# One list orders every engine: the same 2710 steps in a new order

## The chip, the cores and the metric

The kernel runs on one core of a Trainium2 chip. The metric is the device time of one execution in microseconds; lower is better. A core has a matrix engine (TensorE, PE in the profile, with PEld for its weight loads), VectorE (DVE), ScalarE (ACT), GpSimd (POOL), and SyncE (SP), which here only issues DMAs. Each engine works through its own queue in the order in which the program names its instructions, and waits at the first one whose inputs or buffers are not ready.

## The reference

Two parts run one after the other. The first is a gated recurrence (an mLSTM) over 768 positions for 4 batches and 8 heads of width 40. Per step it computes

```python
m_new  = np.maximum(f_gate[:, :, t] + m, i_gate[:, :, t])
f_stab = np.exp(f_gate[:, :, t] + m - m_new)
i_stab = np.exp(i_gate[:, :, t] - m_new)
C = f_stab * C + i_stab * outer(v_t, k_t)
n = f_stab * n + i_stab * k_t
y[:, :, t] = sigmoid(o_gate_t) * (C @ q_t) / np.maximum(np.abs(n . q_t), 1.0)
```

The second is a gated feed-forward layer (FFN) on the 3072 tokens of width 320: `(sigmoid(x @ w_gate) * (x @ w_val)) @ w_out`, with 1536 hidden units. The weights arrive as 64-bit floats, the rest as 32-bit floats.

## The kernel before

**Tiles and stages.** The recurrence is computed in 6 chunks of 128 positions. A chunk of one batch is a *unit*; units 0 to 23 are numbered chunk by chunk, four batches each (`unit`, L507). A unit loads q, k, v and the output gate (`lq`, `lk`, `lv`, `lo`) and, from unit 2 on, a decay table (`ld`); turns q and k with PE (`tr`); forms the scores of its heads (`s`, in three groups); multiplies them with the decay table on DVE (`t`); multiplies with V (`av`); adds the contribution of the earlier chunks (`in`, `ti`, `ad`); normalizes (`nd`, `ns`, `ro`, `xd`); turns the result (`xt`) and splits it into a high and a low part (`xh` on ACT, `xl` on DVE) for the FFN. All but the last chunk also update the state (`kw`, `cs`, `cm`, `cd`, `ca`).

How scores get their operands depends on the chunk. In chunks 0 and 1, ACT or DVE copies the turned q and k (`cp`), and q is multiplied with a mask into a block form (`qb`). From chunk 2 on (units 8 to 23) both are split (`kh` on ACT, `kl` on DVE), written to DRAM by six DMAs (`sw`) and read back in another arrangement by four (`sr`), and only then can `s` begin.

**The weights** come as 64-bit words and are unpacked: a load (`wd`), one ACT step (`wa`), three DVE steps (`wb`, `wc`, `wo`), then the high part on ACT (`wh`) and the low part on POOL (`wl`). The letter behind says which weight: `g` gate, `v` value, `r` the rest rows of both, `o` output.

**The FFN** (`ffn`, L852) has 103 pieces. Each has six matmuls for the gate and six for the value (`u0`, `u1`, L863), two more for each (`r0`, `r1`, L867 and L868), tanh on ACT (`th`), the product on DVE (`gx`), the split (`gh` on ACT, `gl` on DVE), and three down-projection matmuls per token tile (`dn`, L897 to L899). The last piece of a chunk is followed by the output copy and store (`ob`). Gate and value have one accumulation bank each, so the next piece's `u0` waits for `th` and its `u1` for `gx`. Pieces 0 to 15 belong to chunk 0, 16 to 39 to chunk 1, and so on; the last chunk's 24 pieces begin with 79.

**What sets the order.** Every step is a small function under a name such as `u1.14` or `sw9.02`. `ORDER` (L36) is one long list of these names, written out in the program; `emit` calls them in turn, and the engines' queues follow that order (no scheduler reorders them). Some buffers rotate, three each for q, k, v, the output gate and the decay table: which load gets which buffer follows the list as well.

**The start.** Gate values are loaded (`lf` on SP, `li` on ACT's queue), scanned (`ga`, `gb`, `gc`, `gm`) and turned (`tap`, `tac`). `i0` to `i6` make masks on POOL. `wm` is 16 warm-up matmuls on zeros. `lq0` is the one q load that ACT's queue issues; all other loads are SP's. Units 0 and 1 get their decay table from PE (`sp`), ACT (`ee`) and POOL (`em`).

Of the kernel before, what the change touches and what calls it, by code (L numbers as in the profile page):

```python
# [13 lines left out]
ALU = mybir.AluOpType  # L14
# [27 lines left out]
    tr2.1 wbo0 xd0 cp2.1 wbo1 wco1 qb2.1 whg0 nd1 wdv1 ns1 wco0 cm0.1 xt0 xh0 ro1 ld3 qb2.0 woo0 xd1 lq3 woo1 ee2.0
    xt1 xl0 wdg1 lo2 lo3 who0 wlg0 xh1 xl1 u0.0 gm4 gm5 r0.0 who1 ee3.1 wlo1 u1.0 th0 wdo2 kw1 r1.0 cs1 wlo0 wag1
    wbg1 og3 tr2.2 gs1 wao2 wdr1 lq5 lv2 wav1 l12 gx0 gh0 cm1.0 cm1.1 wcg1 zs1 gl0 wbv1 wog1 wbo2 gd whg1 em2 wco2
    lk3 ld4 dl2 kw2 u0.1 u1.1 tr3.0 wdg2 cp2.2 tr3.2 lv5 qb2.2 cp3.0 tr3.1 cp3.2 og2 cp3.1 qb3.0 wlg1 s2.1 s2.0 woo2
    who2 tab t2.1 r0.1 wlo2 war1 wag2 l13 zs0 t2.0 tbp tbc lk4 r1.1 dn0.1 qb3.1 wcv1 wbr1 zs2 th1 s2.2 t2.2 cs2
    cm2.1 cm2.0 av2 dn0.0 gx1 gh1 wov1 whv1 wlv1 qb3.2 lo6 wcr1 wbg2 tdp wor1 tdc wdo3 u0.2 ld5 wdv2 nd2 wao3 ns2
    tep gl1 dn1.1 s3.1 dn1.0 ro2 xd2 ee3.0 em3 wbo3 u1.2 wco3 whr1 dl3 wlr1 wdr2 woo3 who3 wlo3 tec t3.1 ee4.1 s3.2
    lq4 ee4.0 s3.0 war2 t3.2 wcg2 r0.2 t3.0 wog2 th2 r1.2 xt2 xh2 xl2 av3 whg2 wbr2 kw3 wlg2 gx2 ns3 gh2 tr4.0 wav2
    u0.3 nd3 ro3 u1.3 r1.3 xd3 gl2 cp4.0 r0.3 wdv3 th3 wbv2 qb4.0 gx3 wdo4 xt3 cs3 xh3 gh3 dn2.0 xl3 cm3.0 cm3.1  # L50
    u0.4 u1.4 wao4 r0.4 r1.4 wcv2 gl3 wov2 dn2.1 whv2 dn3.0 th4 dn3.1 u0.5 wcr2 wor2 lo4 og4 wlv2 gx4 tr4.2 gh4
    ee5.0 gl4 tr4.1 wdg3 lk5 wbo4 whr2 r0.5 u1.5 wco4 r1.5 wdo5 th5 cp4.1 dn4.2 em4 dl4 wlr2 gx5 woo4 gh5 lq6 lv6
    gl5 u0.6 dn4.3 wao5 wbo5 wco5 r0.6 cp4.2 wdr3 th6 who4 wlo4 u1.6 r1.6 qb4.2 dn5.2 wav3 woo5 dn5.3 s4.0 lv4 l14
    kw4 gx6 who5 gh6 wlo5 wbv3 u1.7 u0.7 r0.7 r1.7 wag3 l15 gl6 th7 wcv3 cs4 gx7 wdg4 wov3 dn6.2 war3 dn6.3 wbg3
    whv3 wbr3 t4.0 wlv3 cm4.1 cm4.0 u0.8 u1.8 ld6 s4.2 r0.8 gh7 ee6.1 gl7 ee6.0 wcg3 qb4.1 wdg5 th8 s4.1 t4.2 in4
    wog3 wdo7 r1.8 wcr3 wao7 whg3 ti4 wlg3 ee5.1 gx8 gh8 t4.1 u0.9 dn7.3 tr5.0 lk6 wdv4 wav4 cp5.0 u1.9 tr5.1 wbo7
    wco7 woo7 lk7 who7 tr5.2 wor3 wdo6 gl8 dn7.2 cp5.1 dn8.1 whr3 r0.9 av4 wlo7 r1.9 wbv4 cd4.1 th9 gx9 u0.10 cd4.0
    em5 ad4 ns4 gh9 qb5.1 lq8 dn8.0 nd4 dn8.3 cp5.2 wlr3 wao6 r0.10 wag4 u1.10 wdo8 qb5.0 gl9 dn9.0 dn9.1 dn9.3
    r1.10 ca4.0 wcv4 gs3 wbo6 wco6 qb5.2 ro4 xd4 dn8.2 dn9.2 gs4 wov4 woo6 th10 wbg4 u0.11 gs2 r0.11 whv4 gs5 wlv4
    gx10 gh10 ca4.1 xt4 gl10 dl5 xh4 who6 wlo6 wdr4 u1.11 r1.11 wcg4 th11 wog4 whg4 s5.1 war4 dn10.0 xl4 s5.2 gx11  # L60
    t5.1 wao8 wlg4 wbo8 dn10.3 wbr4 u0.12 wcr4 s5.0 wor4 wco8 woo8 whr4 wag5 gh11 dn10.2 who8 wlr4 u1.12 wbg5 r0.12
    kw5 r1.12 gl11 lq7 dn10.1 t5.2 in5 wlo8 wcg5 th12 wog5 wdr5 wdo9 gx12 u0.13 em6 dl6 wao9 dn11.1 ti5 u1.13 lo5
    og5 r0.13 wdv5 og6 war5 dn11.2 gh12 whg5 wbr5 r1.13 wlg5 ld7 gl12 ee7.0 t5.0 th13 dn12.2 wcr5 tr6.0 wor5 av5
    wav5 wbo9 wco9 woo9 whr5 dn12.1 cp6.0 cd5.1 qb6.0 wlr5 tr6.1 wbv5 wcv5 wov5 l16 ad5 dn11.0 who9 u0.14 dn12.0
    cp6.1 nd5 wdo11 qb6.1 whv5 ns5 cs5 cm5.1 gx13 wlv5 r0.14 cm5.0 dn11.3 gh13 wlo9 s6.1 dn12.3 gl13 wao11 tr6.2
    t6.1 wdo10 lv7 wao10 th14 wbo10 wbo11 cd5.0 cp6.2 ro5 xd5 u1.14 r1.14 gx14 wco10 woo10 u0.15 gh14 wco11 dn13.0
# [10 lines left out]
    t8.2 t8.0 lo9 r0.22 s8.1 t8.1 th22 dn21.0 r1.22 cd7.1 ca7.1 gx22 xt7 lq10 ob0.3 dl9 xh7 xl7 tr9.2 u0.23 lk10 vb8
    kh9.2 sw9.12 kl9.2 r0.23 gh22 u1.23 r1.23 gl22 in8 dn22.0 th23 gx23 sw9.01 qk9.2 ti8 u0.24 sw9.10 av8.0 da8 db8
    sw9.11 av8.1 av8.2 ad8 cs8 cm8.1 sw9.00 sr9.10 sr9.01 sr9.11 sr9.00 cm8.0 r0.24 ld11 nd8 u1.24 ns8 lk11 dn21.1
    dn22.1 tr10.0 gh23 tr10.1 r1.24 gl23 dn23.0 th24 gx24 dn23.1 kh10.0 kl10.0 kh10.1 sw10.02 ob0.2 kl10.1 u0.25  # L80
    r0.25 u1.25 r1.25 gh24 ea10 qk10.0 kw9 gl24 th25 tr10.2 l19 dn24.1 qk10.1 gx25 u0.26 u1.26 i4 kh10.2 qk10.2
# [869 lines left out]
```

## Time and profile before

| what | value |
|---|---|
| median of 3 runs | 557.59 us (554.11 to 567.98) |
| the profiled execution, whole | 555.66 us |
| its span, first to last instruction | 553.7 us |
| PE busy | 530.0 us, 96% of the span |
| PE weight loads busy | 485.6 us, 88% |
| DVE, ACT, POOL busy | 328.0, 230.1, 246.8 us |
| granted PE clock, mean | 0.99 |
| DMA moved | 72.34 MB, mean 131 GB/s |

The page is one profiled execution. Its second part cuts the span in 40 slices of 13.84 us; a digit is the busy share of a slice in tenths. A line of the chain of waits is a start, a duration and what ran; a line of the waits is who waited for whom, the sum in us, how many times, and the longest one. Matmuls overlap in the array, so busy time of PE counts a matmul's whole passage, not its pace.

### The profile page before, as it was taken

Reading aid. Unit: us, or ns where it says so; the run is one execution under the profiler, and the core shown is the slowest. Engines: PE = TensorE matmul, PEld = TensorE weight load, DVE = VectorE, ACT = ScalarE, POOL = GpSimd, SP = SyncE. Lnnn points to the kernel's source line nnn. Section 1 sums busy time; section 2 is a strip of 40 time slices with the busy share of each in tenths; the row PEclk is TensorE's granted clock in tenths of the full one; section 3 lists DMA queues with packets and bytes.
Section 4 is the critical chain, followed back from the end, with each engine's and each line's share of the span. In section 5 each row is a group of like instructions: output and inputs, shape, how many; then the busy total and the mean of one; then the engine's idle time right before and its main releaser. Section 6 shows DMA issues by size and latency. Waiting matters only on the chain.

```text
span 553.7 us, 10954 instructions
## 1 busy us (share of the span) xinstructions
PE 530.0 (96%) x4101; PEld 485.6 (88%) x4101; DVE 328.0 (59%) x734; ACT 230.1 (42%) x580; POOL 246.8 (45%) x293
## 2 busy tenths in 40 slices
PE   7678999999989999999999999999999999999997
...
DVE  5988877865655564764564654667543554543332
...
PEclk9879999999999999999999999999999999999999
DMA  9897573430787446277786537667047674010000
GB/s 205 228 234 211 135 225 73 134 106 22 179 194 184 125 113 126 58 178 203 171 200 120 114 118 161 177 168 181 25 133 154 147 183 115 27 26 25 25 1 24
DMA packets 131644, 72.34 MB, mean 131 GB/s; under 512 B 103112, under 2 KB 120776, under 8 KB 131592
## 3 DMA queue, kind: packets, MB, share of 16 engines
...
q10 hardware_dynamic: 1088, 0.26, 0.3%
...
## 4 chain that ended last, share of the span: by engine, by line
PE 73%; DMA 9%; DVE 7%; ACT 4%; SPq 2%; issue 2%; POOL 1%; ACTq 0%; DVEq 0%; POOLq 0%
PE pg L863 28%; PE po L897 7%; PE po L899 6%; PE po L898 6%; PE pg L867 5%; PE pg L868 5%; PE av L753 4%; DMA qs<-scr 2%; PE s L664 2%; PE in L736 2%; PE pt L638 2%; PE cs L816 2%; DVE gl L887 1%; PE av L760 1%; PE xt L795 1%
## 5 line engine op out<-in xcount | busy, mean ns | idle before, releaser
L863 PE MATMUL pg<-xh,wh 128*128 128x256 f32 (+1 forms) x412 | 106.3, 340 | 2.0 <-ACT sg L873 1.4
L877 DVE SCALAR_TENSOR_TENSOR sg<-sg,pg 128x256 f32<-128x256 f32 (+1 forms) x103 | 54.1, 525 | 89.0 <-PE pg L868 72.9
L863 PE MATMUL pg<-xl,wh 128*128 128x256 f32 (+1 forms) x412 | 101.6, 328 | 0.0
L863 PE MATMUL pg<-xh,wl 128*128 128x256 f32 (+1 forms) x412 | 101.5, 328 | 0.0
L882 ACT ACTIVATE gh<-sg 128x256 fp32r<-128x256 f32 (+1 forms) x103 | 51.8, 502 | 107.2 <-DVE sg L877 80.8
L897 PE MATMUL po<-oh,gh 128*128 128x320 f32 x288 | 95.8, 332 | 0.0
L899 PE MATMUL po<-oh,gl 128*128 128x320 f32 x288 | 89.7, 311 | 1.0 <-DVE gl L887 1.0
L873 ACT ACTIVATE sg<-pg 128x256 f32<-128x256 f32 (+1 forms) x103 | 48.1, 467 | 101.1 <-PE pg L868 61.1
L898 PE MATMUL po<-ol,gh 128*128 128x320 f32 x288 | 89.2, 310 | 0.0
L887 DVE TENSOR_TENSOR gl<-sg,gh 128x256 fp32r<-128x256 f32 (+1 forms) x103 | 67.2, 652 | 36.5 <-ACT gh L882 36.1
L863 PEld LDWEIGHTS pg<-xl,wh 128*128 128x128 f32 x412 | 69.7, 191 | 7.2
L863 PEld LDWEIGHTS pg<-xh,wl 128*128 128x128 f32 x412 | 69.6, 190 | 7.2
L863 PEld LDWEIGHTS pg<-xh,wh 128*128 128x128 f32 x412 | 67.2, 191 | 5.3 <-ACT sg L873 2.3
L867 PE MATMUL pg<-xh,w 128*128 128x256 f32 (+1 forms) x206 | 70.4, 343 | 0.1
L868 PE MATMUL pg<-xl,w 128*128 128x256 f32 (+1 forms) x206 | 67.3, 328 | 0.0
L709 POOL TENSOR_TENSOR dr<-d 128x1024 f32<-128x1024 f32 x16 | 31.7, 1979 | 61.6 <-DVE d L693 61.4
L897 PEld LDWEIGHTS po<-oh,gh 128*128 128x128 f32 x288 | 54.5, 189 | 2.9
L898 PEld LDWEIGHTS po<-ol,gh 128*128 128x128 f32 x288 | 54.4, 189 | 2.9
L899 PEld LDWEIGHTS po<-oh,gl 128*128 128x128 f32 x288 | 54.2, 188 | 1.7 <-DVE gl L887 1.7
L693 DVE TENSOR_TENSOR d<-s,d 128x384 f32<-128x384 f32 (+1 forms) x72 | 35.5, 508 | 28.1 <-PE s L664 22.2
L593 POOL TENSOR_SCALAR_AFFINE_SELECT d<-d 128x1024 f32<-128x1024 f32 x22 | 25.8, 1175 | 45.7 <-ACT d L589 44.9
L585 POOL TENSOR_TENSOR d<-at,d 128x1024 f32<-128x1024 f32 x16 | 31.8, 1995 | 26.7 <-DMA d<-mscr 19.1
...
## 6 DMA issues: line engine op xcount, KB each, us to landing
d<-mscr SPq DMA_DIRECT2D x22, 512.0 KB
...
k<-in_k_dram SPq DMA_DIRECT2D x24, 160.0 KB
o<-in_o_gate_dram SPq DMA_DIRECT2D x24, 160.0 KB
v<-in_v_dram SPq DMA_DIRECT2D x24, 160.0 KB
su_o<-in_moe_w_out_dram SPq DMA_DIRECT2D x12, 320.0 KB
out_dram<-ob SPq DMA_DIRECT2D x24, 160.0 KB
```

Of the source, the lines that this page charges most:

```text
L585: E("ea", n).tensor_tensor(dm[n], a, dm[n], ALU.subtract)
L693: nc.vector.tensor_tensor(y, ps_[n, g][:, :nh, :], y, ALU.mult)
L863: nc.tensor.matmul(p, w[y][:, a, fs], x[c][:, a, n0:n1], start=(i + a == 0), stop=False)
L867: nc.tensor.matmul(pg[n, y], w2[y][:, fs], xh[c][:, 2, n0:n1], start=False, stop=False)
L868: nc.tensor.matmul(pg[n, y], w2[y][:, fs], xl[c][:, 2, n0:n1], start=False, stop=True)
L873: nc.scalar.activation(s, pg[n, 0], AF.Tanh, scale=0.5)
L877: nc.vector.scalar_tensor_tensor(sgs[n], sgs[n], 1.0, pg[n, 1], ALU.add, ALU.mult)
L882: nc.scalar.activation(ghs[n][:, :nt], sgs[n], AF.Copy)
L887: E("gl", n).tensor_tensor(gls[n][:, :nt], sgs[n], ghs[n][:, :nt].bitcast(F32), ALU.subtract)
L897: nc.tensor.matmul(p, ghs[n][:, ts], oh[:, j, :], start=(j == 0), stop=False)
L898: nc.tensor.matmul(p, ghs[n][:, ts], ol[:, j, :], start=False, stop=False)
L899: nc.tensor.matmul(p, gls[n][:, ts], oh[:, j, :], start=False, stop=(j == NF - 1))
```

## The change

The list is replaced by another one. It holds the same names, each once; what differs is where they stand. The first lines of the old and the new list, and later stretches:

```diff
-    i3 lf li wz lk0 i1 wm lq0 wdv0 i2 ga tap tr0.2 tr0.0 lo1 i0 lq1 gm0 sp1.0 cp0.0 cp0.2 sp0.0 i6 gb tac ee1.0
-    tr0.1 sp0.1 i5 gc qb0.0 em1.0 gm1 gm2 gm3 cp0.1 ee0.0 em0.0 ee0.1 em0.1 lk1 tr1.1 tr1.0 wdr0 lk2 gs0 cp1.0 wav0
-    war0 wdg0 cp1.1 sp1.1 qb0.2 s0.2 tr1.2 qb1.1 ee1.1 lv0 l10 qb1.0 dl0 t0.2 kw0 cp1.2 lq2 s0.0 qb0.1 wag0 s1.0
...
-    xh6 xl6 gl18 r1.19 ee9 tr9.1 dn18.0 sr8.10 sr8.11 th19 u0.20 gx19 r0.20 u1.20 r1.20 kh9.0 kl9.0 sr8.01 kh9.1
...
-    qk11.1 gx32 cm9.1 lk12 da10 u0.33 lv11 lv10 r0.33 u1.33 r1.33 lv12 in10 gh32 gl32 ro9 th33 tr11.2 xd9 gx33
...
-    s23.2 ns22 dn77.3 xt21 xh21 r1.78 dn77.0 t23.2 xl21 dn76.2 da23 th78 u0.79 dn77.1 gx78 r0.79 in23 gh78 nd22 ro22
...
-    dn101.3 dn101.2 gh102 gl102 dn102.3 dn102.2 ob5.3 ob5.2
+    i6 wz li lf i0 wdo0 wao0 wdr0 i3 i2 lq0 lk1 ga gm0 wbo0 wco0 woo0 lq1 wdv0 tap tac sp0.0 war0 i1 gb sp1.1 tr1.1
+    who0 ee0.0 wav0 em0.0 wbr0 gc tr1.0 gm1 wcr0 lk0 cp1.0 cp1.1 qb1.1 lo0 wdo2 tr1.2 zs2 wbv0 cp1.2 gm2 wlo0 wao2
+    lv0 l10 lv1 sp1.0 zs1 gs0 zs0 wor0 ee1.0 em1.0 ee1.1 em1.1 tr0.1 tr0.0 cp0.0 cp0.1 og0 lq3 qb1.0 lk2 sp0.1 tr0.2
+    cp0.2 ee0.1 wcv0 wdg0 em0.1 s1.1 wm ld2 lo2 gm3 gm4 qb0.1 lq2 qb0.0 s0.0 s0.1 qb0.2 s1.0 wbo2 whr0 qb1.2 s0.2
...
+    gl17 cs7 th18 gx18 xh6 xl6 sw8.02 lk10 lv10 gh18 u0.19 r0.19 cm7.0 cd7.0 tr9.0 u1.19 gl18 th19 ea9 r1.19 dn17.0
...
+    gl21 dn21.1 em8 dl8 kw8 u1.22 r1.22 th22 s8.2 t8.2 in8 ti8 cd8.0 dn21.0 s8.1 gx22 gh22 gl22 u0.23 r0.23 em9
...
+    sw23.10 gh77 gl77 u1.78 sw23.00 s22.0 t22.0 u0.78 lo21 og21 av21.0 av21.1 av21.2 ad21 da22 xt20 ns21 dn77.1 lo23
+    nd21 r1.78 xh20 dn77.2 r0.78 th78 ro21 xl20 xd21 dn77.3 sw23.01 xt21 gx78 xh21 xl21 gh78 in22 ti22 dn77.0 vb22
...
+    dn98.2 gh99 gl99 th100 gx100 gh100 dn99.3 gl100 u0.101 r0.101 th101 u1.101 r1.101 dn99.2 gx101 u0.102 gh101
+    r0.102 u1.102 r1.102 dn100.2 dn100.3 gl101 dn101.3 dn101.2 th102 gx102 gh102 gl102 dn102.3 ob5.3 dn102.2 ob5.2
```

Beside the list, the diff adds two parameters and code for another way to move q, k and the FFN's input through DRAM. Its branches are entered for chunks from the parameter on, and both parameters equal the number of chunks:

```diff
+    'QT': 6,
+    'XT': 6,
...
+        bounced = c >= PARAM["QT"]
+        xbounced = c >= PARAM["XT"]
...
-    if PARAM["V32"] < NCH - 1:
+    if PARAM["V32"] + 1 < PARAM["QT"]:
...
+    scq = [dram.tile([2 * DM + 2, L], F32, name=f"scq{n}", tag=f"scq{n}") for n in range(2)]
+    scx = [dram.tile([DM, L], F32, name=f"scx{n}", tag=f"scx{n}") for n in range(2)]
+    rsign = const.tile([P, 6], F32, name="rsign")
...
+        if bounced:
...
-        if not stacked:
+        elif not stacked:
```

More of the change, by code (lines that the diff above doesn't have):

```diff
@@ L42 @@
[L42 to L66, printed above, removed]
@@ L77 @@
[L77 to L81, printed above, removed]
@@ new lines @@
+    r1.1 gl0 th1 dn0.0 t2.2 wdg2 t2.0 gx1 s2.1 ld3 gh1 tr3.2 cp3.2 u0.2 t2.1 war1 wbr1 tbp tbc wag2 wbg2 ee3.1 wcr1
+    gl1 av2 ee3.0 lv4 lo3 cs2 qb3.0 wcg2 wog2 wdo3 wao3 dn0.1 ns2 nd2 em3 dn1.1 ld4 cm2.0 wbo3 wco3 wor1 og3 cm2.1
+    tdp lk4 tdc l13 dn1.0 gs2 dl3 tep ee4.1 ro2 wdv2 xd2 whr1 s3.0 qb3.2 tec wlr1 t3.0 whg2 woo3 wlg2 u1.2 s3.2 s3.1
+    r0.2 th2 t3.2 xt2 xh2 t3.1 xl2 kw3 r1.2 gx2 av3 who3 wlo3 wdr2 war2 wbr2 tr4.0 ns3 u1.3 ee4.0 r1.3 wdv3 nd3 ro3
+    xd3 gh2 gl2 u0.3 r0.3 wav2 th3 xt3 dn2.0 cp4.0 qb4.0 dn2.1 wbv2 xh3 wcv2 cs3 wcr2 gx3 xl3 u1.4 wdo4 wao4 wor2
@@ new lines @@
+    qk17.2 gx58 dn57.1 kl17.2 ca15.0 s16.0 u1.59 r1.59 kl17.1 sw17.12 sw17.11 sw17.10 s16.2 gh58 gl58 dn58.1 dl16
+    t16.2 t16.0 l116 dn57.0 va17 lo16 r0.59 in16 ea17 ee17 ti16 cd16.0 dn57.2 dn58.2 kw16 lo17 dn57.3 s16.1 t16.1
+    da16 th59 gx59 gh59 db16 gl59 cs16 cm16.0 u0.60 r0.60 u1.60 tr18.0 th60 cm16.1 dn58.3 r1.60 og16 u0.61 ca16.0
+    dn59.2 tr18.1 dn59.1 va16 lo18 kh18.0 sr17.10 kl18.0 kh18.1 kl18.1 em17 qk18.0 dl17 sr17.01 qk18.1 gx60 sr17.00
+    dn59.3 dn58.0 dn59.0 gh60 cd16.1 gl60 tr18.2 vb16 av16.0 lk19 av16.1 av16.2 kh18.2 sw18.12 sr17.11 ad16 kl18.2
@@ new lines @@
+    av19.2 ad19 nd19 dn64.2 ns19 u0.66 ro19 lq22 xd19 kw19 ld21 r0.66 ea20 dn64.3 th66 xt19 xh19 dn65.3 gx66 xl19
+    gh66 ca17.1 cs19 lq20 cm19.0 gl66 u1.67 u0.67 cd19.1 dn66.3 r0.67 r1.67 dn65.2 dn66.2 ob3.2 th67 lq21 gx67
+    dn65.1 dn66.1 dn65.0 dn66.0 cm19.1 gh67 lo20 tr20.0 u0.68 r0.68 ob3.0 gl67 u1.68 lv20 r1.68 th68 ob3.3 gx68
+    u0.69 ee20 kh20.0 kl20.0 qk20.0 dn67.3 r0.69 dn67.0 lv22 ob3.1 gh68 tr20.1 l122 ca19.1 kh20.1 kl20.1 sw20.02
+    qk20.1 tr20.2 kh20.2 qk20.2 sw20.00 kl20.2 sw20.01 sw20.10 sw20.11 u1.69 r1.69 cs18 cm18.1 lk21 dn67.1 gl68 th69
@@ new lines @@
+    gx82 gh82 gl82 u0.84 r0.84 u1.84 r1.84 th84 gx84 dn82.1 dn83.1 dn82.0 dn83.0 u0.85 r0.85 u1.85 r1.85 gh84 gl84
+    th85 u0.86 r0.86 dn84.1 dn84.0 gx85 u1.86 gh85 r1.86 gl85 th86 dn85.0 dn85.1 gx86 gh86 u0.87 r0.87 u1.87 r1.87
+    gl86 dn86.0 th87 dn86.1 u0.88 gx87 r0.88 gh87 u1.88 gl87 r1.88 dn87.0 th88 dn87.1 u0.89 r0.89 gx88 u1.89 r1.89
+    xh23 xl23 gh88 gl88 th89 dn88.0 dn88.1 u0.90 r0.90 gx89 u1.90 r1.90 gh89 gl89 th90 gx90 dn89.1 u0.91 dn89.0
+    r0.91 u1.91 r1.91 gh90 gl90 dn90.1 th91 gx91 gh91 gl91 dn90.0 u0.93 ob5.0 r0.93 u1.93 r1.93 dn91.2 th93 ob5.1
@@ L334, in _ @@
                                 fill=0.0, base=-(L - 1), channel_multiplier=1)
+    if PARAM["QT"] < NCH:
+        @op("i7")
+        def _():
+            w = rsign[:, 1:4]
+            nc.gpsimd.memset(w, 1.0)
+            nc.gpsimd.affine_select(out=w, in_=w, pattern=[[-DX, 3]], compare_op=ALU.is_ge,
+                                    fill=0.0, base=0, channel_multiplier=1)
+            nc.gpsimd.affine_select(out=w, in_=w, pattern=[[DX, 3]], compare_op=ALU.is_ge,
+                                    fill=0.0, base=D - 1, channel_multiplier=-1)
+            m = rsign[:, 0:1]
+            nc.gpsimd.tensor_tensor(m, w[:, 0:1], w[:, 1:2], ALU.add)
+            nc.gpsimd.tensor_tensor(m, m, w[:, 2:3], ALU.add)
+            nc.gpsimd.tensor_scalar(rsign[:, 4:6], w[:, 1:3], -2.0, m, ALU.mult, ALU.add)
+        @op("i8")
+        def _():
+            for n in range(2):
+                nc.sync.dma_start(scq[n][2 * DM :], warm[:2, :L])
     @op("wm")
@@ L594, in _, with turned_out @@
                                         fill=0.0, base=0, channel_multiplier=-1)
-        if not stacked:
+        def turned_out(name, dst, src):
+            dv = dst.rearrange("(n j) t -> j n t", j=32)
+            for a in range(4):
+                @op(f"{name}{n}.{a}")
+                def _(a=a):
+                    ts = slice(32 * a, 32 * a + 32)
+                    nc.sync.dma_start(dv[:, :, ts], src()[ts].rearrange("j (n i) -> j n i", i=32))
+        if bounced:
+            sc = scq[b % 2]
+            @op(f"tq{n}")
+            def _():
+                split[n] = t = sbt("kh", [P, 2, DM], F32, f"tq_{n}")
+                for x, y in enumerate((qt, kt)):
+                    nc.vector.transpose(t[:, x, :], y[n].rearrange("p h d -> p (h d)"))
+            turned_out("tw", sc[: 2 * DM], lambda: split[n].rearrange("p x d -> p (x d)"))
+            for x, y in ((1, "k"), (0, "q")):
+                for i in range(3):
+                    @op(f"sr{n}.{x}{i}")
+                    def _(x=x, y=y, i=i):
+                        if (n, x) not in stk:
+                            stk[n, x] = sbt("bl" if x == 0 else "bh", [P, 9, L], F32R, f"{y}s_{n}")[:, :H]
+                        src = sc[x * DM : x * DM + DM].rearrange("(h d) t -> d h t", d=D)
+                        src = bass.AP(tensor=src.tensor, offset=src.offset, ap=[[src.ap[0][0], DX]] + [list(z) for z in src.ap[1:]])
+                        nc.sync.dma_start(stk[n, x][i * DX : (i + 1) * DX].bitcast(F32), src)
+                @op(f"sh{n}.{x}")
+                def _(x=x, y=y):
+                    r = 3 * DX
+                    sgn[n, x] = t = sbt("st", [P, H, L], F32, f"{y}t_{n}", 3)
+                    nc.scalar.activation(t[:r].bitcast(F32R), stk[n, x][:r].bitcast(F32), AF.Copy, scale=rsign[:r, 5 - x : 6 - x])
+                @op(f"sl{n}.{x}")
+                def _(x=x):
+                    r = 3 * DX
+                    R = stk[n, x]
+                    nc.vector.scalar_tensor_tensor(R[:r], R[:r].bitcast(F32), rsign[:r, 3 - x : 4 - x], sgn[n, x][:r], ALU.mult, ALU.add)
+            for y in range(2):
+                @op(f"sq{n}.{y}")
+                def _(y=y):
+                    r = 3 * D
+                    if y == 0:
+                        qk[n] = sbt("qk", [P, 3, L], F32, f"qk_{n}", 2)
+                        nc.sync.dma_start(qk[n][:r, :2], sc[: 2 * r].rearrange("(g r) t -> r g t", r=r))
+                    else:
+                        nc.sync.dma_start(qk[n][: 2 * D, 2], sc[2 * r : DM])
+            for g, (h0, nh) in enumerate(GROUPS):
+                @op(f"s{n}.{g}")
+                def _(g=g, h0=h0, nh=nh):
+                    ps_[n, g] = p = pst("pa", [P, 3, L], f"s_{n}_{g}")
+                    for m in range(nh):
+                        nc.tensor.matmul(p[:, m, :], stk[n, 1][: 3 * DX, h0 + m, :], stk[n, 0][: 3 * DX, h0 + m, :], start=True, stop=True)
+        elif not stacked:
```

248 lines of the change are left out of this document (133 added, 115 removed).

## The prediction

> **What bounds the kernel now.** I read the page first: span, busy time, the slices.
>
> ```profile
> span 553.7 us, 10954 instructions
> ...
> PE 530.0 (96%) x4101; PEld 485.6 (88%) x4101; DVE 328.0 (59%) x734; ACT 230.1 (42%) x580; POOL 246.8 (45%) x293
> ...
> PE   7678999999989999999999999999999999999997
> ...
> DVE  5988877865655564764564654667543554543332
> ...
> PEclk9879999999999999999999999999999999999999
> DMA  9897573430787446277786537667047674010000
> ```
>
> TensorE (PE) is the bound from the fourth slice (13.84 us each) to the end. In the first three it has gaps, VectorE (DVE) and the DMA engines are nearly full, and the only dip of the granted clock lies there. So I asked for busy time by stage, cut where the start is over: where the transposes of the fourth unit's result (`xt3`) begin, after which PE runs nearly closed.
>
> ```profile
> 57.30 0.57 PE L795 MATMUL xt<-ident,x 128*128 128x128 f32 x3
> ```
>
> ```profile
> 0.00:13.50 13.50, 10.52 (x61) 10.11 (x62) 7.01 (x18) 5.61 (x17) 5.10 (x19) 1.00 1.01 204
> 13.50:57.30 43.80, 35.05 (x220) 28.55 (x219) 39.17 (x92) 31.33 (x91) 29.13 (x37) 0.88 0.89 228
> 57.30:540.00 482.70, 474.11 (x3747) 436.85 (x3746) 277.94 (x617) 189.77 (x466) 212.58 (x239) 1.00 0.50 123
> 540.00:553.70 13.70, 10.34 (x81) 10.07 (x79) 3.88 (x9) 3.35 (x9) 0.00 (x0) 0.97 0.07 24
> ```
>
> The columns are the length of the stage, then PE, PEld, DVE, ACT and POOL busy, clock, DMA share, GB/s. PE is idle 13.50 − 10.52 = 3.0 us in the first stage, 8.7 us in the second, 8.6 us in the long middle and 3.4 us at the end: together 23.7 us, which is 553.7 − 530.0. Between 13.5 and 57.3 DVE is busy 39.2 of 43.8 us, so there DVE, not PE, sets the pace; DMA at 0.89 is close behind.
>
> No instruction is added or removed, so PE's 530 us stay. A new list can only win part of the 23.7 us, or add to them. The profiled execution took 555.7 us, 2.0 us more than its span and 0.3% under the median of 557.6 us; sums below are against 555.7.
>
> One caution on the word busy. [...]
>
> ```profile
> 316.37 1.36 PE pg L863 x6
> ```
>
> Six 512-wide matmuls advance the chain by 1.36 us, 227 ns each, so a matmul recorded longer than that can cover a short wait.
>
> **The change, part by part.** The old and new lists hold the same 2710 names, and the two new parameters equal the number of chunks, so the added branches are never taken. What is left is another order in each engine's queue.
>
> *The end.* The last six down-projection steps follow the last gate-and-value step in both lists, `ob5.2` last. The 3.4 us stay: 0.
>
> *The middle.* The waits of PE between 60 and 540 us, largest first of those that a list can move, and the chain around them:
>
> ```profile
> PE s L664 <- DMA qs<-scr: 2.9, 2, 1.8
> ...
> PE cs L816 <- DMA v<-in_v_dram: 1.1, 1, 1.1
> PE po L899 <- DVE gl L887: 1.0, 1, 1.0
> ```
>
> ```profile
> 146.18 3.71 DMA scr<-kl
> ...
> 151.24 6.74 DMA qs<-scr
> ...
> 158.25 0.74 PE s L664 x5
> ...
> 202.11 4.71 DMA v<-in_v_dram
> ...
> 206.96 0.80 PE cs L816 x6
> ...
> 333.20 7.01 DMA qs<-scr
> ...
> 340.56 0.75 PE s L664 x5
> ```
>
> The scores `s8` and `s16` wait for keys and queries that go out to DRAM (3.7 us) and come back rearranged (6.7 to 7.0 us). They are covered by PE work between the unit's last transpose (`tr`) and its first `s`. Counted with the chain's own rates (1.36 us for six 512-wide matmuls, half that for 256-wide), the old list has 13.0 us there for unit 8 and 15.8 for unit 16; the new one has 15.3 and 23.3. Both waits, 2.9 us, should go: unit 8 needed 13.0 + 1.8 = 14.8 us, unit 16 needed 15.8 + 1.1 = 16.9. For unit 8 the cover is only just enough, and what is late next is the same step of unit 18, with 16.7 us in the new list. The wait of `cs10` for V goes too (1.1 us): in the old run V's load starts at 202.11 us and lands after 4.7 us, in the new list `lv10` stands right behind `lk10`, near the transposes of unit 9 and far ahead of `cs10`. The wait on `gl` is an instruction that ran long; no position removes it: 0. Sum −4.0.
>
> New waits: `xt21` stands only 2.6 us of PE work behind `av21`, and the first FFN step of the last chunk (`u0.79`) only 1.0 us behind `xt21`. The nearest rows:
>
> ```profile
> 308.83 1.23 PE av L753 x48
> ...
> 313.31 0.34 PE xt L795 x3
> ...
> 314.52 1.39 PE pg L863 x6
> ```
>
> Here unit 15 needed 313.31 − 310.06 = 3.2 us from the end of `av` to `xt`, and 0.9 us from the end of `xt` to FFN work sufficed. So the new list lacks up to 0.6 us at `xt21`. With an equal shortage at `xt19` (2.7 us of work) that makes +1.2. Bounds: 0, since the 3.2 us in the old trace was PE's own queue and not a wait, to +3. I take 1.2. Middle: −2.8.
>
> *The start.* The new list loads and unpacks output weights first (`wdo0`, `wao0`, `wbo0`...) and loads `k0` eighth on SyncE's (SP) queue instead of second; the warm-up matmuls (`wm`) move from PE's first place to behind `s1.1`.
>
> ```profile
> k<-in_k_dram SPq DMA_DIRECT2D x24, 160.0 KB
> ...
> su_o<-in_moe_w_out_dram SPq DMA_DIRECT2D x12, 320.0 KB
> ...
> q<-in_q_dram SPq DMA_DIRECT2D x23, 160.0 KB
> st_v<-in_moe_w_val_dram SPq DMA_DIRECT2D x6, 512.0 KB
> ...
> su_r<-in_moe_w_gate_dram SPq DMA_DIRECT2D x6, 128.0 KB
> ...
> gin<-in_f_gate_dram SPq DMA_DIRECT2D x1, 96.0 KB
> ```
>
> ```profile
> 1.26 5.71 DMA q<-in_q_dram
> ```
>
> ```profile
> 3.70 0.41 DVE L345 TENSOR_TENSOR_SCAN gin<-bmask,gin 32x128 f32<-32x128 f32 x1 [2.50 <-POOL ident masks.py:199]
> ```
>
> ```profile
> 1.26 3.78 PE L340 MATMUL pwarm<-warm 128*128 128x128 f32 x16 [1.26 <-DVE warm L277]
> ...
> 7.87 3.01 PE L552 MATMUL mb<-m,ident 128*128 128x128 f32 x16
> ...
> 14.66 3.65 PE L629 MATMUL s<-qbd,qkt 120*128 120x384 f32 x10 [0.68 <-ACT qkt L615]
> ...
> 29.15 0.80 PE L863 MATMUL pg<-xh,wh 128*128 128x256 f32 x2 [0.58 <-ACT xh L802]
> ```
>
> In the old run `q0` has landed at 6.97 us and scores start at 14.66. In the new list two gate loads, `wdo0`, both halves of `wdr0`, `k1`, `q0`, `q1` and `wdv0` are queued ahead of `k0`: with it 2 × 96 + 320 + 2 × 128 + 4 × 160 + 512 = 1,920 KB. At 204 GB/s that is 9.6 us, so `k0` lands near 11 to 12 us. Also `lq0` stands on ScalarE's (ACT) queue behind `wao0`, which waits for a 320 KB load. No row shows a DMA issue behind a waiting ACT instruction: if it isn't held up, `q0` lands at 7 us as now; if it is, at about 6 + 5.7 = 12 us. Either way `k0` decides. Unit 0's scores then need its masked copies on DVE, which now stand behind weight steps and gate scans: 23 DVE instructions from the second scan to `qb0.0`, at 39.17 / 92 = 0.43 us each 9.8 us, from 7 us (first weight landed) with 1 to 2 us of waiting. That puts `s0.0` at 18 to 19 us, 4 later. From there to `xl0`, which the first FFN step needs, it is 31 DVE instructions, 13.2 us, and about 1.5 us of waiting: first FFN matmul at 34 us, 5 later than 29.15.
>
> That is not lost. DVE is the pacer, and the set of its steps ahead of `xt3` is the same in both lists, except that `gx3` and `wbv2` (2 × 0.43 = 0.9 us) come after it in the new one. `xt3` can come later only if DVE idles more. It idled 6.5 us before 13.5 and 4.6 us until 57.3. In the new list it unpacks weights from about 7 us on; I count idle until the gates' scan at 3.70 (3.4 us, as now), 1.7 us for the first weight load, about 1 for unit 1's first V weights, 1 for `s0.2` and the old 4.6 later: 11.7 against 11.1. With 0.9 less work: −0.3, so 0. Bounds: −4, if the later idle goes (five loads fewer, `wdo4` among them, and one V load more stand ahead of `xt3`), to +7, if the 5 us are not won back and PE starts the FFN cold.
>
> The clock, in a row of its own:
>
> ```profile
> 23.70:34.10 10.40, 6.90 (x31) 5.91 (x31) 9.92 (x23) 7.90 (x22) 8.03 (x10) 0.51 0.92 232
> ```
>
> PE ran at half clock from 23.7 to 34.1 us, after a thin stretch, and again at the very start (16 mask matmuls in 3.01 us, even with the warm-up ahead). In the new list the thin stretch moves to about 20 to 34 us and the FFN again starts cold: the same loss, 0. [...]
>
> Sum: 555.7 − 2.8 + 0 + 0 = 552.9. Forecast 553 us.
>
> **The rivals.**
>
> *Faster, about 541.* The orders were drawn from real durations, and also the small waits fit: all 8.6 us of middle idle go, and DVE's idle at the start falls from 11 to about 5 us (for it: it has weights to work on from 7 us). 555.7 − 8.6 − 6 = 541. Against it: most single middle waits are under 1 us and come from stretched DVE steps, which no list foresees. Chance 0.20.
>
> *Slower, about 564.* One mechanism: the late `k0`. Everything in unit 0 and 1 follows it in order on PE, so DVE runs out of weight steps before attention steps are released. It decides when the first FFN matmul starts later than about 35 us with DVE idle in between: then each microsecond is lost for good, because after 57.3 us PE has almost no idle time to catch up in. Price: 5 us from the late start, 2 to 3 from PE's cold clock over the FFN steps that then set the end, no gain in the middle: 555.7 + 8 = 564. It passes 2% (568.8) only when the first FFN matmul starts after about 40 us. Chance 0.17, about half of it above 2%.
>
> *An even trade, 555.7.* The waits only change places: unit 8's cover is just 0.5 us more than it needed, unit 18's is less than unit 16 needed, and `xt21` and `xt19` are shorter than before. Chance 0.20.
>
> **How the numbers follow.** The forecast has 0.43. Range 542 to 564: the low end takes in most of the fast rival, the upper the slow one up to its price, leaving out about 0.2. Two per cent, about what a measurement here can tell from no change, is 546.4 and 568.8 against the median. Faster by over 2%: nearly all of the fast rival, 0.18, and 0.02 of the forecast's tail. Slower by over 2%: 0.10. Within: 0.70.
>
> **What would show it.** Right: `xt3` begins between 55 and 60 us though the first FFN matmul is later than 32; no wait of `s` for the DRAM round trip over 1 us; `cs10` not waiting; PE idle between the start and 540 us near 6 us. Wrong: DVE idle over 14 us before `xt3`, `xt3` after 62 us (slow rival), or a middle with over 9 us of PE idle in new places (even trade). PE's busy sum away from 530 us would mean that the queue order changes the matmuls' own pace, which none of my terms has.

## The result and the profile after

| | before | after |
|---|---|---|
| median | 557.05 us (551.91 to 567.98, 20 runs) | 550.31 us (548.23 to 555.15, 20 runs) |
| the profiled execution, whole | 555.66 us | 548.54 us |
| its span | 553.7 us | 546.8 us |

The ratio is 0.992, with a 95% interval of 0.989 to 0.995: a gain, and a small one. The forecast was 553.

The page of the changed kernel: span, busy time, and the slices, now 13.67 us each.

```profile
span 546.8 us, 10945 instructions
...
PE 528.0 (97%) x4101; PEld 485.5 (89%) x4101; DVE 332.1 (61%) x734; ACT 229.7 (42%) x580; POOL 245.4 (45%) x293
...
PE   5689999999999999999999999999999999999997
...
DVE  6878796977667557645576744657443355653322
...
PEclk9879999999999999999999999999999999999999
```

PE starts weaker (5, 6, 8 where before had 7, 6, 7) and DVE stronger at first: weights are unpacked while the attention operands are still under way. The middle is closed as before. The same stages as in the prediction, cut where the transposes of unit 3 (`xt3`) begin; columns are length, then PE, PEld, DVE, ACT and POOL busy, clock, DMA share, GB/s.

```profile
0.00:13.50 13.50, 7.59 (x45) 6.49 (x45) 8.87 (x21) 5.12 (x12) 6.81 (x19) 1.00 0.92 204
13.50:56.70 43.20, 36.96 (x233) 31.80 (x234) 35.53 (x90) 30.96 (x94) 27.26 (x38) 0.88 0.79 204
56.70:540.00 483.30, 479.97 (x3802) 443.96 (x3801) 286.34 (x622) 192.41 (x471) 211.30 (x239) 1.00 0.51 125
540.00:546.80 6.80, 3.52 (x26) 3.25 (x24) 1.36 (x4) 1.24 (x3) 0.00 (x0) 1.00 0.13 48
```

PE's idle time up to `xt3` is 5.9 + 6.2 = 12.1 us (11.7 before), in the middle 3.3 us (8.6 before), at the end 3.3 us (3.4 before). So the span's 6.9 us split like this: `xt3` comes 0.6 us sooner, PE idles 5.3 us less after it, and its busy time after it is 1.0 us shorter.

The start, in rows of the timeline of PE: the first transposes of unit 0's q and k, the first scores (unit 1's, `s1.1`), the first FFN matmul, `xt3`.

```profile
10.51 0.30 PE L689 MATMUL pt<-ident,q 128*120 128x128 f32 x1 [0.69 <-DMA q<-in_q_dram]
11.18 0.32 PE L689 MATMUL pt<-ident,k 128*120 128x128 f32 x1 [0.37 <-DMA k<-in_k_dram]
...
15.20 0.88 PE L712 MATMUL s<-qbd,qkt 120*128 120x384 f32 x2 [2.01 <-ACT d L586]
...
35.08 0.51 PE L966 MATMUL pg<-xh,wh 128*128 128x256 f32 x2 [0.58 <-ACT xh L905]
```

```profile
56.72 0.49 PE L898 MATMUL xt<-ident,x 128*128 128x128 f32 x3
```

The first FFN matmul is 5.9 us later than before (29.15), and `xt3` is not later at all. All waits of PE in the middle (who waited for whom, sum in us, times, longest):

```profile
PE av L836 <- DVE qk L740: 1.1, 1, 1.1
PE pg L966 <- DVE sg L980: 0.6, 1, 0.6
PE pt L721 <- DVE qk L740: 0.6, 1, 0.6
PE pt L689 <- DVE t L851: 0.5, 1, 0.5
PE av L843 <- DVE d L776: 0.3, 1, 0.3
```

The waits of `s` for the DRAM round trip, of `cs10` for V and of `dn28.2` for `gl28` are not among them. One of 1.1 us is new: `av8.0` for DVE.

### The profile page after: what moved, and what is told of

It is laid out like the page before. It is cut to its first block, busy times and chain, and to the rows that moved or that the text cites. A ratio compares the mean times of both kernels' runs of the same rounds, so it can differ in the third digit from the quotient of the medians.

```text
span 546.8 us, 10945 instructions
## 1 busy us (share of the span) xinstructions
PE 528.0 (97%) x4101; PEld 485.5 (89%) x4101; DVE 332.1 (61%) x734; ACT 229.7 (42%) x580; POOL 245.4 (45%) x293
## 4 chain that ended last, share of the span: by engine, by line
PE 86%; DVE 5%; ACT 3%; DMA 2%; issue 2%; POOL 1%; SPq 1%; ACTq 0%; DVEq 0%; POOLq 0%
PE pg L966 35%; PE po L1000 7%; PE po L1002 7%; PE po L1001 7%; PE pg L970 6%; PE pg L971 6%; PE av L836 4%; PE s L747 2%; PE in L819 2%; PE cs L919 2%; PE av L843 2%; PE pt L721 2%; PE s L712 2%; PE xt L898 1%; DMA st_v<-in_moe_w_val_dram 1%
## 5 line engine op out<-in xcount | busy, mean ns | idle before, releaser
L990 DVE TENSOR_TENSOR gl<-sg,gh 128x256 fp32r<-128x256 f32 (+1 forms) x103 | 64.9, 630 | 39.4 <-ACT gh L985 39.3
L971 PEld LDWEIGHTS pg<-xl,w 128*128 128x128 f32 x206 | 39.1, 190 | 2.5
```

Of the source, the lines that this page charges most:

```text
L971: nc.tensor.matmul(pg[n, y], w2[y][:, fs], xl[c][:, 2, n0:n1], start=False, stop=True)
L990: E("gl", n).tensor_tensor(gls[n][:, :nt], sgs[n], ghs[n][:, :nt].bitcast(F32), ALU.subtract)
```

## The experiments

Two questions: which part of the list gains, the start up to `xt3` or the rest; and what the new wait is.

**The old list in the new program.** It tests that the added code does nothing.

```diff
 ORDER = """
-    i6 wz li lf i0 wdo0 wao0 wdr0 i3 i2 lq0 lk1 ga gm0 wbo0 wco0 woo0 lq1 wdv0 tap tac sp0.0 war0 i1 gb sp1.1 tr1.1
...
+    i3 lf li wz lk0 i1 wm lq0 wdv0 i2 ga tap tr0.2 tr0.0 lo1 i0 lq1 gm0 sp1.0 cp0.0 cp0.2 sp0.0 i6 gb tac ee1.0
...
```

> The changed program with the old list put back: the added parameters, tiles and unused branches stay, the order is the old one. Theory (only the order acts): the time of the kernel before, ratio 0.997 to 1.003, first FFN matmul near 29 us, `xt3` near 57 us. Rival (the added tiles move buffers in memory and that matters): it keeps part of the gain of 0.8%, ratio 0.992 to 0.996.

559.43 us median, ratio 1.000 (0.996 to 1.004). The list is the change. In the profiled execution `xt3` came at 59.8 us and not near 57; the clock was at half for 15.0 us ahead of it, not 10.2 (table below).

**The new start with the old order of the rest.**

```diff
     xd3 gh2 gl2 u0.3 r0.3 wav2 th3 xt3
-    dn2.0 cp4.0 qb4.0 dn2.1 wbv2 xh3 wcv2 cs3 wcr2 gx3 xl3 u1.4 wdo4 wao4 wor2
...
+    lq5 lv5 lo6 ld5 cp4.0 wbv2 qb4.0 gx3 wdo4 cs3 xh3 gh3 dn2.0 xl3 cm3.0 cm3.1
...
```

> The kernel before, with the new list up to and with `xt3` and then the old list's order of all that is left. Theory (the start only trades places, the gain lies in the middle): first FFN matmul near 35 us, `xt3` near 57 us, the scores' waits for the DRAM round trip (2.9 us) and the V wait (1.1 us) are back, time within 0.3% of before, ratio 0.997 to 1.003. Rival (the start is what gains): ratio 0.990 to 0.994.

560.00 us median, ratio 1.005 (1.002 to 1.008): nothing gained, and 2 us lost, which neither theory had. The waits of PE after 57 us in its profile:

```profile
PE pt L638 <- DVE qk L657: 2.0, 3, 1.3
PE pg L863 <- ACT sg L873: 1.9, 4, 0.8
PE s L664 <- DMA qs<-scr: 1.2, 2, 0.8
...
PE po L899 <- DVE gl L887: 1.0, 1, 1.0
PE cs L816 <- DMA v<-in_v_dram: 1.0, 1, 1.0
```

The three waits of the old rest are back, the one for the round trip with 1.2 us instead of 2.9. A new one of 1.3 us stands at `tr8.2` (147.44 us). The trace shows what delayed it: a DVE step of 0.17 us (`nd7`) took 1.80 and ended 0.07 us after a GpSimd step.

```profile
144.56 1.80 DVE L773 TENSOR_SCALAR den<-t 128x8 f32<-128x8 f32 x1
```

```profile
144.39 1.90 POOL L585 TENSOR_TENSOR d<-at,d 128x1024 f32<-128x1024 f32 x1 [5.60 <-DMA d<-mscr]
```

Why such a pair matters is the subject of the last experiments.

**The old start with the new order of the rest.** The old list up to `xt3`, without the nine steps that the new list puts later, then the new list's order. A first hybrid kept these nine steps ahead of `xt3` and gave no time: in that order the engines wait for each other for good, a deadlock. Why was not looked into.

```diff
-    wbg1 og3 tr2.2 gs1 wao2 wdr1 lq5 lv2 wav1
+    wbg1 og3 tr2.2 gs1 wao2 wdr1 lv2 wav1
...
-    u0.3 nd3 ro3 u1.3 r1.3 xd3 gl2 cp4.0 r0.3 wdv3 th3 wbv2 qb4.0 gx3 wdo4 xt3 cs3 xh3 gh3 dn2.0 xl3 cm3.0 cm3.1
...
+    u1.3 r1.3 xd3 gl2 r0.3 wdv3 th3 xt3 gs4 lv4 gs2 dn2.0 cp4.0 qb4.0 dn2.1 wbv2 xh3 wcv2 cs3 wcr2 gx3 xl3 u1.4 wdo4
...
```

> The kernel before with the old list up to the transposes of unit 3 (less nine steps that the new list puts later: lq5, lv5, lo6, ld5, cp4.0, wbv2, qb4.0, gx3, wdo4) and the new list's order for all that follows. Theory (the gain is made after the start): ratio to the kernel before 0.989 to 0.994, first FFN matmul near 29 us as before, xt3 near 57, no wait of s for the DRAM round trip, PE idle from xt3 to 540 us of 3 to 5 us against 8.6. Rival (the new start is what counts): ratio 0.997 to 1.003.

548.61 us median, ratio 0.980 (0.976 to 0.985). The gain lies in the rest, and is larger than expected. That this hybrid is no slower than the changed kernel was not expected by either theory, so both ran again side by side on one chip:

> The changed kernel itself, beside the two hybrids that follow, so that the start is judged on one chip. Theory (the new order of the rest gains, the new start costs): ratio to the kernel before 0.988 to 0.994, and 0.2 to 0.6% above the hybrid with the old start. Rival (the two starts are worth the same; the hybrid's 0.980 came from that chip): both within 0.2% of each other.

> The same kernel as the hybrid of the old start and the new rest measured before. Theory: ratio 0.982 to 0.989, and below the changed kernel on this chip by 0.2 to 0.6%. Rival: within 0.2% of the changed kernel.

Changed kernel 550.76 us (549.80 to 556.67), ratio 0.990 (0.984 to 0.996); hybrid 549.01 us (547.39 to 552.18), ratio 0.985 (0.981 to 0.989). By the medians the hybrid is 0.3% ahead, as the theory had it; the intervals overlap, so this is likely and not settled. The hybrid's stages:

```profile
0.00:55.40 55.40, 45.71 (x278) 38.68 (x279) 46.27 (x110) 37.04 (x106) 34.35 (x55) 0.91 0.90 210
55.40:540.00 484.60, 480.88 (x3811) 444.42 (x3810) 286.29 (x623) 192.89 (x472) 211.05 (x239) 1.00 0.51 125
```

Profiles of these kernels, cut at the start of `xt3`; "half clock" is the time up to `xt3` at which the granted clock was 0.5:

| kernel | `xt3` at | half clock until then | `xt3` to end |
|---|---|---|---|
| before | 57.3 | 10.2 | 496.4 |
| old list in the new program | 59.8 | 15.0 | 499.6 |
| new start, old rest | 57.9 | 13.7 | 498.8 |
| changed | 56.7 | 10.2 | 490.1 |
| changed, again | 58.4 | 13.7 | 491.2 |
| old start, new rest | 60.8 | 23.9 | 491.7 |
| old start, new rest, again | 55.4 | 10.2 | 490.3 |

Every kernel here with the new order of the rest needs 490 to 492 us after `xt3` (the variants below 489 to 493), with the old order 496 to 500. The start varies with the clock it happens to get. At the same 10.2 us of half clock it is 57.3, 56.7 and 55.4: the new list's start is worth next to nothing.

**Three waits moved in the old list**: `s8.0` and `s8.2` behind `u0.22`, three down-projections ahead of `s16.1`, and the V load `lv10` ahead of `lk12`.

```diff
-    sw9.02 r0.21 dn19.0 th21 u1.21 r1.21 gx21 dn20.1 gh21 s8.0 gl21 lq11 s8.2 em9 em8 xd7 u1.22 dn20.0 dl8 kw8 u0.22
+    sw9.02 r0.21 dn19.0 th21 u1.21 r1.21 gx21 dn20.1 gh21 gl21 lq11 em9 em8 xd7 u1.22 dn20.0 dl8 kw8 u0.22 s8.0 s8.2
...
-    qk11.1 gx32 cm9.1 lk12 da10 u0.33 lv11 lv10 r0.33
+    qk11.1 gx32 cm9.1 lv10 lk12 da10 u0.33 lv11 r0.33
...
-    kl17.2 s16.1 sw17.01 dl16 th59 t16.1 s16.2 dn57.0 dn58.0 kw16 dn57.3 t16.2
+    kl17.2 dn57.0 dn58.0 dn57.3 s16.1 sw17.01 dl16 th59 t16.1 s16.2 kw16 t16.2
```

> The kernel before with eight names moved: `s8.0` and `s8.2` behind `u0.22` (1.9 us more PE work ahead of them), `dn57.0`, `dn58.0`, `dn57.3` ahead of `s16.1` (1.35 us more), and V's load for unit 10 ahead of that for unit 11 and of `lk12`, the buffers of the two swapped. Theory (each wait costs what PE idles there, and the prediction's 4.0 us can be had alone): the waits of `s8` and `cs10` fall under 0.3 us and that of `s16` too, span 553.7 - 4.0 = 549.7 us, ratio 0.991 to 0.995. Rival (even trade: a wait removed comes back at the next short cover): span 552 to 554, ratio 0.997 to 1.001.

553.86 us median, ratio 0.994 (0.990 to 0.997). Its waits after 57 us:

```profile
PE s L664 <- DVE d L693: 1.9, 3, 0.9
PE pg L863 <- ACT sg L873: 1.4, 2, 0.9
PE s L664 <- DMA qs<-scr: 1.1, 2, 0.7
PE po L899 <- DVE gl L887: 1.0, 1, 1.0
```

By the medians, three small moves bring over half of what the whole new list brings, as the theory had it. The profile does not show where: its span is 553.7 us, that of the kernel before and what the rival had, with `xt3` 0.8 us later. PE idles 7.5 us between `xt3` and 540 us instead of 8.6. The waits of `s8` for the round trip and of `cs10` for V are gone, but `s16.1` still waits 0.75 us (1.11 before), and scores now wait for DVE, 1.9 us in three places. Why the medians differ by 4 us all the same is taken up at the end and stays open in part.

**q0 and k0 early in the new list.** Does the late `k0` cost anything?

```diff
-    i6 wz li lf i0 wdo0 wao0 wdr0 i3 i2 lq0 lk1 ga gm0
+    i6 wz li lq0 lf lk0 i0 wdo0 wao0 wdr0 i3 i2 lk1 ga gm0
...
-    who0 ee0.0 wav0 em0.0 wbr0 gc tr1.0 gm1 wcr0 lk0 cp1.0 cp1.1
+    who0 ee0.0 wav0 em0.0 wbr0 gc tr1.0 gm1 wcr0 cp1.0 cp1.1
```

> The changed kernel with the load of k0 right behind the gate load lf on SyncE's queue, and that of q0 right behind the gate load li on ScalarE's queue, so that neither waits for output weights. Theory (VectorE paces the start, its set of steps is the same): the first transposes at 8 to 9 us instead of 10.5, the first scores at 15 to 16.5 instead of 17.9, but xt3 still within 1 us of 56.7, and the time within 0.3% of the changed kernel, that is a ratio of 0.989 to 0.995 to the kernel before. Rival (late k0 costs the start): xt3 2 us or more earlier and a ratio of 0.984 to 0.989.

550.91 us median (549.84 to 551.40), ratio 0.985 (0.981 to 0.989), no better than the changed kernel by the medians. The ratio lies in the rival's range, but the earlier `xt3` that the rival named did not come: it stands at 59.6. Nor did the edit make unit 0's transposes earlier, the 10.5 us of the expectation. Unit 1's stand ahead of them in PE's queue; they began at 8.05 us in the changed kernel and here, where `q1` comes later, at 9.38. The rows are unit 1's and unit 0's first:

```profile
9.38 0.47 PE L689 MATMUL pt<-ident,q 128*120 128x128 f32 x1 [0.59 <-DMA q<-in_q_dram]
...
11.33 0.27 PE L689 MATMUL pt<-ident,q 128*120 128x128 f32 x1
```

The scores of unit 0 began at 20.8 us instead of 17.9. Of these 2.9 us, 1.5 are the warm-up matmuls ahead of them, which took 3.41 us instead of 1.95 while the clock was at half. DVE, too, is behind, as the first 8 us show, here of this kernel and then of the changed one (DVE is the third busy time):

```profile
0.00:8.00 8.00, 3.28 (x15) 3.17 (x16) 1.80 (x6) 1.77 (x2) 3.38 (x15) 1.00 0.89 175
```

```profile
0.00:8.00 8.00, 3.65 (x17) 3.36 (x17) 4.54 (x12) 3.64 (x8) 3.62 (x16) 1.00 0.83 177
```

With q0 and k0 ahead of the first weight load, DVE does 2.7 us less in this stretch and wins back 1.7 of it by 20 us (11.26 us busy from 8 to 20 instead of 9.52). Part of the later `xt3` is the clock, which was at half for 13.6 us ahead of it; the changed kernel with 13.7 us of that (table above) has `xt3` at 58.4. So q0 and k0 ahead of the first weights cost the start about 1 us; what sooner transposes of unit 0 would bring was not reached by this edit.

**The masks early.** In the changed kernel `av1` waits 1.5 us, by the profile for the head masks that GpSimd makes late (`i5`).

```diff
-    sp0.0 war0 i1 gb sp1.1 tr1.1
+    sp0.0 war0 i1 i5 gb sp1.1
...
-    ro0 t1.0 qb2.2 i5 tr2.1 em2
+    ro0 t1.0 qb2.2 tr2.1 em2
```

> The changed kernel with the head masks rmask (i5, 0.44 us on GpSimd) made right behind i1, where GpSimd is idle, so that av1 does not wait 1.5 us for them. Theory (VectorE paces the start): av1 earlier by 1 to 1.5 us, xt3 within 0.7 us of 56.7, the time within 0.2% of the changed kernel. Rival (a wait of TensorE in the start costs its length): xt3 1 us or more earlier and the time 0.2 to 0.3% lower.

550.49 us median, beside 550.76 for the changed kernel on that chip; ratio 0.988 (0.983 to 0.993). Nothing was gained, `xt3` came at 58.2, and `av1` did not begin earlier. Its row on PE, and DVE's last step ahead of it:

```profile
27.45 2.41 PE L843 MATMUL av<-v,d 128*128 128x41 f32 x16 [1.53 <-POOL qbd L705]
```

```profile
26.80 0.54 DVE L776 TENSOR_TENSOR d<-s,d 128x384 f32<-128x384 f32 x1
```

The profile now names another GpSimd step, which had ended at 26.54. The masks are not among the inputs of `av1`. What it reads is `t1.0`, and DVE ended that at 27.34, just ahead of 27.45. In the changed kernel it is the same: `t1.0` ends at 26.85, `av1` begins at 26.94. So the experiment rested on a releaser that the profile names and that is not the one; the wait was for DVE, the pacer, from the start.

**The new wait of `av8.0`.** Its place in the changed kernel, from the timeline:

```profile
166.86 0.32 POOL L930 TENSOR_TENSOR cst<-cst,cdec 80x82 f32<-80x82 f32 x1
...
166.94 2.38 DVE L990 TENSOR_TENSOR gl<-sg,gh 128x256 fp32r<-128x256 f32 x1 [0.54 <-ACT gh L985]
...
167.14 1.89 POOL L611 TENSOR_TENSOR d<-at,d 128x1024 f32<-128x1024 f32 x1
...
169.57 0.28 DVE L740 COPY qk<-pt 120x128 f32<-120x128 f32 x1
...
169.90 0.20 PE L836 MATMUL av<-v,d 128*128 128x41 bf16 x1 [1.07 <-DVE qk L740]
```

`gl24`, a step of 0.4 to 0.5 us, took 2.38 us and ended 0.29 us after a GpSimd step with two inputs (`ea10`). Behind it in DVE's queue stood `qk10.0`, for which PE waited. To see whether GpSimd is the cause, `ea10` is moved, and with it `ee10`, the ScalarE step that reads its result:

```diff
-    u0.25 cd8.1 r0.25 ea10 kl10.0 qk10.0 xt7 av8.0
+    u0.25 cd8.1 r0.25 kl10.0 qk10.0 xt7 av8.0
...
-    r0.26 u1.26 ee10 dn24.0
+    r0.26 u1.26 dn24.0
...
-    ro8 s9.2 th28 xd8 tr10.2
+    ro8 s9.2 th28 xd8 ea10 ee10 tr10.2
```

> The changed kernel with GpSimd's ea10 and ScalarE's ee10 moved behind xd8, so that no two-input GpSimd step lies beside gl24. Theory: gl24 takes at most 0.9 us instead of 2.38, qk10.0 behind it in VectorE's queue is on time, and av8.0 waits under 0.3 us for VectorE instead of 1.1. Rival (gl24 is long whatever GpSimd does): gl24 still takes over 2 us and av8.0 still waits about 1 us.

`gl24` took 0.52 us and the wait of `av8.0` was gone:

```profile
168.15 0.52 DVE L990 TENSOR_TENSOR gl<-sg,gh 128x256 fp32r<-128x256 f32 x1 [0.54 <-ACT gh L985]
```

The cause is shown: `gl24` takes 2.38 us in all six profiles with the new order of the rest and `ea10` unmoved and whole, 0.52 and 0.53 in the two with `ea10` moved. The single execution took 550.16 us; to see what it is worth, the same move was made in the hybrid:

> The hybrid of the old start and the new rest, with GpSimd's ea10 and ScalarE's ee10 moved behind xd8. Theory (the stretched gl24 costs what av8.0 waits for it): the wait of av for qk of 1.1 us goes, and the time falls by 0.5 to 1.1 us, 0.1 to 0.2%, against the hybrid. Rival (another wait takes its place): no gain, and a new wait of about 1 us between 165 and 220 us.

548.75 us median, beside 549.01 for the hybrid without it; ratio 0.984 (0.979 to 0.988). The wait of `av8.0` is gone, and as the rival had it, others took its place, at `dn28.2` (181 us) and `cs9` (198 us). Whether time was gained is open: one of the six executions took 558.03 us, and without it the median is 547.95, 1.1 us under the hybrid's.

```profile
PE po L896 <- ACT gh L881: 0.9, 1, 0.9
...
PE cs L815 <- DVE qk L656: 0.3, 1, 0.3
```

**GpSimd's two-input steps in halves**, so that DVE would be held up for half as long:

```diff
-                E("ea", n).tensor_tensor(dm[n], a, dm[n], ALU.subtract)
+                for hs_ in (slice(0, 4), slice(4, H)):
+                    E("ea", n).tensor_tensor(dm[n][:, hs_], a[:, hs_], dm[n][:, hs_], ALU.subtract)
...
```

`da` and `db` are split in the same way.

> The changed kernel with GpSimd's steps ea, da and db (one 128x1024 two-input operation each) split in two halves of 128x512 each. Theory (a VectorE gl that runs long is one that ends only when GpSimd's two-input step ends): the longest gl falls from 2.38 us to under 1.5, the wait of av for qk (1.1 us, at 170 us) falls to under 0.4, GpSimd's busy time rises by 2 to 6 us, and the time changes by 0 to -1.5 us against the changed kernel (ratio to the kernel before 0.987 to 0.994). Rival (gl runs long for another reason): the longest gl stays at 2 us or more and the wait stays.

Neither theory held as a whole. 555.29 us median, ratio 0.993 (0.990 to 0.997): 4 to 5 us slower than the changed kernel was on other chips. GpSimd's busy time rose by 5.8 us, as expected, and the wait of `av8.0` went. But the longest `gl` is now 3.39 us, not under 1.5, and a state update on DVE shows why. In the halved kernel, DVE, GpSimd and PE near 210 us:

```profile
208.28 5.44 DVE L950 TENSOR_TENSOR cst<-cst,ct 120x246 f32<-120x246 f32 x1
```

```profile
208.36 1.09 POOL L620 TENSOR_SCALAR_AFFINE_SELECT d<-d 128x1024 f32<-128x1024 f32 x1
209.41 2.04 POOL L794 TENSOR_TENSOR dr<-d 128x512 f32<-128x512 f32 x2
211.41 2.03 POOL L799 TENSOR_TENSOR ds<-dr 128x512 bf16<-128x512 f32 x2
```

```profile
214.30 0.51 PE L969 MATMUL pg<-xh,wh 128*128 128x256 f32 x2 [2.73 <-DVE sg L983]
```

The same place in the changed kernel, DVE and GpSimd:

```profile
208.10 3.30 DVE L947 TENSOR_TENSOR cst<-cst,ct 120x246 f32<-120x246 f32 x1
```

```profile
208.18 1.09 POOL L619 TENSOR_SCALAR_AFFINE_SELECT d<-d 128x1024 f32<-128x1024 f32 x1
209.24 1.89 POOL L792 TENSOR_TENSOR dr<-d 128x1024 f32<-128x1024 f32 x1
211.21 1.95 POOL L796 TENSOR_TENSOR ds<-dr 128x1024 bf16<-128x1024 f32 x1
```

There is a pause of 0.08 us between GpSimd's second and third step in the changed kernel, and DVE's step, whose median is 0.4 us, ends 0.19 us after the third began. In the halved kernel the steps follow each other with no pause, and DVE's step is held to the end of the whole row. So at this place DVE's step followed not the length of one GpSimd step but how long GpSimd went on without a pause: it ended 0.27 us after the pause at 211.13 began in the changed kernel, and 0.28 us after the row's end at 213.44 in the halved one. PE's wait there grew from 0.6 to 2.7 us; a second one, behind the 3.39 us `gl47`, cost 1.6 us. With the wait of `av8.0` gone, PE idles 5.4 us after `xt3` instead of 3.3; that is 2 of the 4 to 5 us, and the others stay open.

## Why the prediction was right or wrong

**The direction, and the place of the gain: right.** Forecast −2.8 us in the middle, 0 at the start and at the end; the profiles show −5.3 us of idle time after `xt3`, −0.6 us at the start and −0.1 us of idle at the end, and the two hybrids place the gain after `xt3`.

**The three waits, −4.0: right.** All are gone. The trace has 15.3 us between unit 8's last transpose and its first scores, as counted, and 23.0 for unit 16 (23.3). "For unit 8 the cover is only just enough" holds to the letter: of nine profiles with the new order of the rest, six show no wait there, and three show 0.6, 1.0 and 1.1 us at `s8.2`. Unit 18, named as next late, never waited in them.

**New waits at `xt21` and `xt19`, +1.2: wrong.** No profile has a wait there. The 3.2 us that unit 15 needed in the old trace was PE's own queue, as the lower bound said, and the lower bound was the one to take.

**`gl`, 0, "an instruction that ran long; no position removes it": the sum was right by luck, the reason wrong.** Its position beside a two-input step of GpSimd is what makes it long, and the list sets that; for `gl24` a run shows it (2.38 us beside `ea10`, 0.52 without), for `gl28` only its place in the trace (2.15 us, begun 0.02 us after a GpSimd step of 1.89). The new list takes `gl28` out of such a place (−1.0) and puts `gl24` into one, which costs `av8.0` 1.1 us. Two changes that the working did not have cancel.

**Small waits: not in the sum.** The other waits after `xt3` fell from 3.6 us to 2.2. These 1.4 us, the 1.2 that did not come and PE's busy time, 1.0 us shorter after `xt3`, less 0.1 for `av8.0` against `gl28`, make the 3.5 us by which the working's −2.8 fell short of the −6.3 in the profile. "PE's 530 us stay" was 2 us off; why the matmuls' own records are shorter was not tested.

**The start, 0, because DVE paces it: right.** `k0` landed at 11.2 us (forecast 11 to 12), unit 0's scores began at 17.9 (18 to 19), the first FFN matmul came at 35.1 (34), and `xt3` at 56.7, inside the 55 to 60 that was named as the sign. DVE idled 12.3 us until then (forecast 11.7). The half-clock stretch moved from 23.8 to 24.5 us and kept its 10.2 us, as forecast. No run shows the 2 to 3 us that the slow rival added for PE's cold clock, an estimate of the author's; what the profile showed is this same 10.2 us. That PE ran at half clock at the very start too is read from the pace alone: the clock column stands at 1.00 for the first 13.5 us, but the 16 warm-up matmuls took 3.78 us there, and 1.95 in the changed kernel, where they begin at 15.9 us. The experiments on single steps agree: weights later on DVE cost the start about 1 us, and the wait of `av1` proved to be one for DVE. The slow rival's late `k0` made PE wait 0.7 us for `q0` and 0.4 for `k0`, and `xt3` was no later. One open point is settled: `lq0` was held up on ScalarE's queue behind `wao0`, was issued at 4.46 us instead of 1.26, and unit 0's transposes waited for it until 10.5. By the hybrids the new start may even cost 1 to 2 us against the old one.

**The size: too small.** A gain of 2.8 us was forecast; 6.7 were measured by the medians and 7.1 by the profiled executions. In the profile, 3.5 of the missing 4.3 us are the terms above, 0.6 the start, and 0.2 lie outside the span. That 553 is only 2.7 us from the measured 550.3 is in part luck: the working counted from the profiled execution of the kernel before, which lies 1.4 us under its median.
